# A fused retention and gated MLP kernel: slot 5's transposes given to the DMA engines, and two rows of O moved into the prologue

## The chip, the core and the metric

The kernel runs on one core of a Trainium2 chip. Five engines work side by side, each through its own queue in order: TensorE (PE in the profile, with its weight loads as PEld), VectorE (DVE), ScalarE (ACT), GpSimd (POOL) and SyncE (SP). Sixteen DMA engines move data. GpSimd issues loads that convert float32 to bfloat16 on the way (the "software queue"); SyncE issues plain loads, stores and DMA transposes (the "hardware queue"). The metric is the device time of one execution in microseconds; the runs' median is compared.

## The reference

Four batches, eight heads, 768 steps, head size 64. A decayed linear attention gives x, which goes through a two-layer network with the activation h·cos(h):

```python
state = gamma * state + k_t^T v_t          # per head, 64 x 64, gamma = 1 - 2**(-5-h)
y_t   = q_t state / sqrt(64)               # x: 3072 tokens x 512
h = x @ w_in                               # 512 -> 2048
out = (h * cos(h)) @ w_out                 # 2048 -> 512
```

## The kernel before

**Slots and blocks.** A slot is a chunk of 128 steps of two batches, all heads; there are 12, and `ORDER` (line 197) starts with the first chunk of both pairs of batches. For each slot q, k and v are loaded (`load`, line 272), scaled by powers of gamma or cast to bfloat16 (`conv_q`, `conv_k`, `conv_v`, lines 320 to 343), and q and k are transposed into `qkt`. The scores are K·Q with a triangular mask (`a_one` line 386 and `a_mm` line 393 on TensorE, `a_mask` line 406 on DVE). The *block* of a slot (`y_block`, line 538) is one dense piece of TensorE work: the state update (line 508), the part of y from the old state (line 494), the part from the masked scores (line 480) and, from slot 4 on, the scores of the *next* slot (line 389). So the transposes of slot p+1 are needed when the block of slot p runs. Inside a block the second half must follow the first; an instruction that does nothing but wait, on an engine given by `hop_on(p)` (line 467: SyncE up to slot 4, GpSimd from slot 5), passes that signal.

**Two ways to transpose.** Up to slot 5 TensorE does it (`t_mm`, line 355, 16 matmuls of line 361 a slot, and copies from PSUM on ACT and DVE, line 365). From `DMA_T = 6` on SyncE issues two DMA transposes a slot (`dma_t`, line 348).

**Groups and units.** Two slots make a group of 512 tokens; 6 groups. A *full unit* (`f_mm`, line 587) is 128 of the 2048 hidden columns for a group: 4 matmuls of 512 columns, then cos on ACT (`f_cos`, line 593), then the multiplication on DVE (`f_mul`, line 600), which frees the PSUM bank. A *half unit* (`h_mm`, line 605) does two column blocks for one slot's 256 tokens in 8 matmuls of 256 columns, so that work can start before the second slot of a group is ready. O is the second layer: a *row* of O (128 tokens) is four *O units* of 4 matmuls (`o_mm`, line 630, matmuls at line 635), a copy on ACT (`o_out`) and a store on SyncE (`o_dma`, line 646). Seven PSUM banks go round in a fixed order; three buffers hold cos.

**Two regimes.** The prologue (lines 704 to 918: slots 0 to 7, groups 0 and 1, O of group 0) is ordered by a small list scheduler, `Plan`, at build time. Each piece of work has the engines that may do it, a cost, what it comes after, and a rank; `SHIFT` moves single ranks, `ON` fixes engines, `HOLD` names engines that may wait for a more urgent piece. The order that it finds is written out for each engine; no time of it exists on the chip. `LOADS` (line 719) is the order of the software queue. `HALF0` (line 168) says how many column blocks of group 0 are done as half units. `CQ`, `CD` say which engine scales slot 2's q and v, `SPLIT` which masks of slots 0 and 1 go by ACT and GpSimd. The names in these tables are those given by `add`: `f0.8` is a full unit, `t50` a transpose, `dt60` a DMA transpose, `m300` a mask, `cq30` a q scaling, `oc0` a store of a row. DMA transposes there come after the load of k7, the last but one of the software queue (line 800).

The loop from line 943 does groups 2 to 5: 16 steps a group, each a full unit of group g and an O unit of group g-1, with a block at steps 3 and 11, followed by the conversions and DMA transposes two slots ahead and SyncE's loads three slots ahead (`load(nc.sync, ...)`, 13 issues a slot, because k and v are loaded with halves exchanged from slot 8 on). The first such load, slot 8's, is issued in the prologue (line 903).

Of the kernel before, what the change touches and what calls it, by code (L numbers as in the profile page):

```python
# [164 lines left out]
HOLD = ""  # L165
# [6 lines left out]
def kernel(  # L172
# [7 lines left out]
    out: bass.AP,  # L180
):
    nc = tc.nc
    B, H, S, D = q.shape
    C = 128
    NC = S // C
    DM = H * D
    DF = moe_w_in.shape[1]
    HP = H // 2
    KIN = DM // 128
    KOUT = DF // 128  # L190
    NP = B // 2 * NC
    NG = NP // 2
    PRE = 5
    NB = 3
    DMA_T = 6

    ORDER = [0, NC] + [x for x in range(1, NP) if x != NC]
    SWAP = 8
    LATE = NC

    scale = 1.0 / math.sqrt(D)
    lg = [math.log(1.0 - 2.0 ** (-5.0 - h)) for h in range(H)]

    ctx.enter_context(tc.manual_schedule())
# [262 lines left out]
    def hop_on(p):  # L467
        return nc.sync if p <= 4 else nc.gpsimd
# [225 lines left out]
    for h in range(H):  # L694
        nc.scalar.activation(out=dec[:, h % 2, h // 2, :], in_=dist, func=AF.Exp, bias=lnsc,
                             scale=float(lg[h]))
    nc.scalar.activation(out=gq, in_=lgp, func=AF.Exp, bias=lnsc)
    nc.scalar.activation(out=gk, in_=lgp, func=AF.Exp, scale=-1.0)
    nc.scalar.activation(out=lnsc, in_=halfpi, func=AF.Sin)
    for i in range(7):  # L700
        idle_mm("E", 2)


    PL = 6
    ASEP = 4
    MERGE = 4
    CQ, CD = "P", "DP"
    SPLIT = {(1, 1, 1), (0, 1, 1)}
    HM, HCQ, HCV = "q2", "", ""
    plan = Plan({"bank": 7, "cos": 3, "sem": 8, "out": 4, "port": 1, "ring": 7}, 6.5)  # L710
    add = plan.add
    SB2 = {"D": (0.33, 0.42), "A": (0.49, 0.585)}
    TT = {"D": (0.6, 0.69), "P": (1.03, 1.05)}
    PS = {"D": (0.6, 0.69), "A": (0.49, 0.585)}
    ld = {}
    prev = None
    at = lambda tm: dict(start=0.0, free=0.0, done=tm, lat=0.0)
    ld["q", 0, 0], ld["q", 0, 1], ld["k", 0, 0], ld["k", 0, 1] = map(at, (3.9, 5.0, 7.4, 7.4))
    LOADS = ["Q1", "K1", "v0", "v1", "w0a", "w0b", "w1", "w2", "q2", "k2", "w3a", "v2", "w3b", "o0", "q3", "k3", "v3", "o1", "q4", "o2", "k4", "v4", "q5", "k5", "o3", "v5", "q6", "k6", "v6", "q7", "k7", "v7"]
# [26 lines left out]
    T = {}  # L746
    G = lambda *k: T.get(k)
    for p in range(PL + 2):
# [26 lines left out]
        if p < DMA_T:  # L775

            for u in range(2):
                cq, ck = ([T["c" + x, p, b] for b in ((u,) if p < 2 else (0, 1))] for x in "qk")
                ev = lambda w, x, need: add("DA", SB2, lambda e, p=p, u=u, w=w: t_copy(p, u, w, e),
                                            need + old, 10 * p + 0.5, (), [("bank", 1)] if w else [],  # L780
                                            name="e%s%d%d" % (x, p, u))
                if p < 2:
                    tq = add("E", 0.225, lambda e, p=p, u=u: t_mm(p, u, 0), cq, 10 * p + 1,
                             [("bank", 1)], (), "full", name="tq%d%d" % (p, u))
                    T["eq", p, u] = ev(0, "q", [tq])
                    tk = add("E", 0.225, lambda e, p=p, u=u: t_mm(p, u, 1), ck + [T["eq", p, u]],
                             10 * p + 1, (), (), "full", name="tk%d%d" % (p, u))
                    T["ek", p, u] = ev(1, "k", [tk])
                else:
                    tq = tk = add("E", 0.45, lambda e, p=p, u=u: (t_mm(p, u, 0), t_mm(p, u, 1)),  # L790
                                  cq + ck, 10 * p + 1, [("bank", 1)], (), "full",
                                  name="t%d%d" % (p, u))
                    T["eq", p, u] = ev(0, "q", [tq])
                    T["ek", p, u] = ev(1, "k", [tk, ("issued", T["eq", p, u])])
                T["tq", p, u], T["tk", p, u] = tq, tk
            kq = {u: [T["eq", p, u], T["ek", p, u]] for u in range(2)}
        else:
            for w, x in enumerate("qk"):
                T["dt", p, w] = add("S", (1.3, 4.6), lambda e, p=p, w=w: dma_t(p, w),
                                    [T["c" + x, p, 0], T["c" + x, p, 1], ld["k", 7, 0]] + old, 10 * p,  # L800
                                    name="dt%d%d" % (p, w))
            kq = {u: [T["dt", p, 0], T["dt", p, 1]] for u in range(2)}
# [81 lines left out]
    for o, x, p in pend:  # L884
        o["after"] += [T[c, p, b] for b in range(2) for c in (("cv", "cd") if x == "v" else ("c" + x,))]
    for x, ops in ((HM, [T[("m",) + x] for x in SPLIT]), (HCQ, [T["cq", 2, b] for b in range(2)]),
                   (HCV, [T["cd", 2, b] for b in range(2)])):
        for o in plan.ops:
            if o["name"] == x:
                o["after"] += ops  # L890
# [52 lines left out]
    for g in range(2, NG + 1):  # L943
        for s in range(16):
            hf, r = divmod(s, 8)
            p = 2 * (g + 1) + hf
            if g < NG:
                if g == 2 and s == 0:
                    o_mm(1, 0, 0)
# [48 lines left out]
```

## Time and profile before

| | |
|---|---|
| median of 3 runs | 209.5 us (209.27 to 209.53) |
| the profiled execution's own time | 208.1 us |
| its span | 206.3 us |
| granted TensorE clock | 1.00 |
| TensorE busy | 201.4 us, 98% |
| DVE, ACT, POOL busy | 55%, 56%, 36% |
| software queue | 15.47 MB, last load issued at 51.0 us, lands 11.5 us later |
| first useful matmul of the MLP | 15.76 us |

Times in the profile count from the start of the span. A line of a timeline reads: start, length, engine, source line, operation, output and inputs, count, and in brackets the idle time before it with what ended it. A line of the chain reads: start, length, what. "SPq" and "POOLq" are the queues of these engines, where DMAs are issued.

### The profile page before, as it was taken

The numbers are of one execution on the slowest core, as the hardware profiler recorded it, in microseconds if no ns is written. First come the engines' busy times: TensorE is split into PE (matmuls) and PEld (weight loads), VectorE is DVE, ScalarE is ACT, GpSimd is POOL, SyncE is SP. The second block draws the span as 40 slices with busy tenths as digits, with TensorE's granted clock in tenths as the row PEclk, the third lists the DMA queues.
The fourth block names the chain that finished last, engine by engine and source line by source line (L and its number), as shares of the span: only waits on it lengthen the run. The fifth ranks groups of instructions, "written<-read, shape, count | busy, mean of one in ns | idle before, by whom it ended". The sixth has DMA issues, their size and how long they took to land.

```text
span 206.3 us, 5229 instructions
## 1 busy us (share of the span) xinstructions
PE 201.4 (98%) x2178; PEld 108.6 (53%) x2178; DVE 114.2 (55%) x194; ACT 115.2 (56%) x193; POOL 73.8 (36%) x77
## 2 busy tenths in 40 slices
PE   7999999999999999999999999999999999999994
PEld 2558656868945545445445445454444444444442
DVE  5589897866996548338338438448442444444000
ACT  7567886859855357547546546554555553554120
POOL 8969979899973004305207005200000000000000
PEclk9999999999999999999999999999999999999999
DMA  7999999999998976876877675501101101110212
GB/s 121 186 262 210 314 241 312 255 342 276 344 312 150 231 158 175 201 193 171 192 177 144 151 193 142 153 0 56 53 1 51 51 3 51 51 51 0 104 53 102
DMA packets 58600, 32.15 MB, mean 156 GB/s; under 512 B 47696, under 2 KB 53072, under 8 KB 58576
## 3 DMA queue, kind: packets, MB, share of 16 engines
q0 software_dynamic: 14352, 15.47, 33.9%
q1 hardware_dynamic: 44080, 16.28, 31.1%
q8 instruction: 17, 0.28, 0.6%
q10 hardware_dynamic: 144, 0.07, 0.1%
q14 instruction: 7, 0.06, 0.1%
HBM read 27.26 MB, written 6.29 MB: 163 GB/s over the span
## 4 chain that ended last, share of the span: by engine, by line
PE 78%; DMA 10%; POOL 7%; DVE 2%; issue 1%; ACT 1%; POOLq 0%; DVEq 0%
PE bank L635 37%; PE bank L590 27%; DMA vf<-in_v_dram 10%; PE bank L611 4%; PE bank L389 2%; PE bank L480 2%; PE bank L655 2%; DVE gt L619 1%; PE st_ps L508 1%; POOL qf L281 1%; POOL kf L281 1%; PE bank L494 1%; PE bank L361 1%; POOL w_in_sb L300 1%; POOL ks L281 1%
## 5 line engine op out<-in xcount | busy, mean ns | idle before, releaser
L598 ACT ACTIVATE cosb<-bank,halfpi 128x512 bf16<-128x512 f32 x96 | 65.6, 690 | 53.2 <-PE bank L590 48.0
L635 PE MATMUL bank<-w_out_sb,gt 128*128 128x512 bf16 x368 | 90.9, 379 | 0.0
L602 DVE TENSOR_TENSOR gt<-bank,cosb 128x512 bf16<-128x512 f32 x72 | 49.1, 690 | 55.8 <-ACT cosb L598 55.7
L590 PE MATMUL bank<-xt,w_in_sb 128*128 128x512 bf16 x288 | 73.2, 379 | 0.0
L635 PEld LDWEIGHTS <-gt 128*128 128x128 bf16 x368 | 35.5, 98 | 42.3 <-issue 0.2
L590 PEld LDWEIGHTS <-w_in_sb 128*128 128x128 bf16 x288 | 27.6, 98 | 32.3
L324 POOL TENSOR_TENSOR qs<-qf,gq 128x512 bf16<-128x512 f32 x18 | 18.5, 1044 | 43.5 <-PE bank L480 22.6
L408 DVE TENSOR_TENSOR am<-bank,mask 128x512 bf16<-128x512 f32 x40 | 24.8, 682 | 4.2 <-PE bank L389 4.2
L313 ACT COPY ob<-bank 128x512 f32<-128x512 f32 (+1 forms) x24 | 14.0, 582 | 16.0 <-PE bank L635 13.9
L611 PE MATMUL bank<-xt,w_in_sb 128*128 128x256 bf16 x192 | 22.3, 273 | 0.0
L611 PEld LDWEIGHTS <-w_in_sb 128*128 128x128 bf16 x192 | 18.5, 98 | 3.1
L619 DVE TENSOR_TENSOR gt<-bank,cosb 128x512 bf16<-128x512 f32 x24 | 16.0, 686 | 4.7 <-ACT cosb L598 4.6
L313 ACT CAST xt<-bank 128x512 bf16<-128x512 f32 x21 | 11.4, 588 | 10.8 <-PE bank L480 10.1
L313 ACT CAST ks<-kf 128x512 bf16<-128x512 f32 x20 | 11.5, 625 | 2.7 <-DMA kf<-in_k_dram 2.7
L664 PE MATMUL bank<-zero 128*128 128x512 bf16 x34 | 10.5, 442 | 1.1 <-DVE halfpi L680 1.1
L480 PE MATMUL bank<-am,vs 64*64 64x128 bf16 (+1 forms) x320 | 10.3, 206 | 0.1
L336 POOL TENSOR_TENSOR vs<-vf,gk 128x512 bf16<-128x512 f32 x8 | 8.9, 1113 | 3.3 <-PE bank L480 1.5
L331 POOL TENSOR_TENSOR vs<-vf,gk 128x512 bf16<-128x512 f32 x8 | 8.2, 1042 | 5.2 <-DMA vf<-in_v_dram 3.8
L281 POOL DMA_DIRECT2D vf<-in_v_dram x8 | 9.4, 1182 | 1.0 <-DVE vs L336 0.8
L315 DVE CAST stb<-st_ps 128x512 bf16<-128x512 f32 x9 | 6.2, 687 | 3.8 <-PE st_ps L508 3.3
L389 PE MATMUL bank<-qkt 64*64 64x128 bf16 (+1 forms) x320 | 8.0, 206 | 0.3 <-ACT qkt L313 0.2
L313 ACT COPY qkt<-bank 128x512 bf16<-128x512 bf16 x13 | 7.1, 592 | 1.8 <-PE bank L361 1.2
(66 smaller groups left out, 132.7 us busy)
## 6 DMA issues: line engine op xcount, KB each, us to landing
out_dram<-ob SPq DMA_DIRECT2D x23, 256.0 KB, 2.4
vf<-in_v_dram POOLq DMA_DIRECT2D x8, 512.0 KB, 12.0
qf<-in_q_dram POOLq DMA_DIRECT2D x6, 512.0 KB, 12.5
kf<-in_k_dram POOLq DMA_DIRECT2D x6, 512.0 KB, 12.4
w_out_sb<-in_moe_w_out_dram POOLq DMA_DIRECT2D x4, 512.0 KB, 14.1
qf<-in_q_dram SPq DMA_DIRECT2D x4, 512.0 KB, 4.6
w_in_sb<-in_moe_w_in_dram POOLq DMA_DIRECT2D x4, 256.0 KB, 8.7
w_in_sb<-in_moe_w_in_dram POOLq DMA_DIRECT2D x2, 512.0 KB, 10.5
```

The source lines that it names most:

```text
L281: eng.dma_start(out=t.rearrange("p b h d -> p (b h) d"), in_=src[ds(2 * bp, 2), :, ds(c * C, C), :].rearrange("b h t d -> t (b h) d"))
L313: nc.scalar.copy(out=out, in_=in_)
L324: ENG[e].tensor_tensor(out=qb(p)[:, b], in0=qf[p % PRE][:, b], in1=bc(gq, ORDER[p] % NC), op=ALU.mult)
L389: return nc.tensor.matmul(ap[b][ts(x, 64), a, lo:], lhsT=kt(p % NB, b, h)[:, ts(x, 64)], rhs=qt(p % NB, b, h)[:, lo:], tile_position=(64 * ...
L408: nc.vector.tensor_tensor(out=am[p % 2][b][u], in0=bank.rearrange("p (a t) -> p a t", a=HP), in1=(dec[:, b] if p < 2 else mask[second(p, 0 ...
L480: m = nc.tensor.matmul(held["yp", p][b][ts(j, 64), a, lo:], lhsT=vs[p % NB][ts(r, 64), b, h, :], rhs=am[p % 2][b][h // 4][ts(r, 64), h % 4 ...
L590: nc.tensor.matmul(bank, lhsT=w_in_sb[:, i, ts(f, 128)], rhs=xt[g % 2][:, i, :], start=(i == 0), stop=(i == KIN - 1))
L598: nc.scalar.activation(out=cb, in_=bank, func=AF.Sin, bias=halfpi)
L602: nc.vector.tensor_tensor(out=gt[g % 2][:, f, :], in0=bank, in1=cb, op=ALU.mult)
L611: nc.tensor.matmul(bank[:, ts(e, 256)], lhsT=w_in_sb[:, i, ts(f + e, 128)], rhs=xt[g % 2][:, i, ts(hf, 256)], start=(i == 0 and e == 0), s ...
L619: nc.vector.tensor_tensor(out=gt[g % 2][:, f : f + 2, ts(hf, 256)], in0=bank.rearrange("p (f t) -> p f t", f=2), in1=cb.rearrange("p (f t) ...
L635: nc.tensor.matmul(bank, lhsT=gt[g % 2][:, f, ts(j, 128)], rhs=w_out_sb[:, f, :], start=(f == 0), stop=(f == KOUT - 1))
```

## The change

Slot 5 is transposed by DMA instead of TensorE (`DMA_T` 5). The DMA transposes of slot p in the prologue come after the load of v of slot p, and the loads of slot p+1 after the issue of these transposes, where they had all come after k7. Two rows of O of group 1 (`ROWS = 2`) become pieces of the prologue's plan, beside the blocks of slots 4 and 5; the loop's first group does the other two, one unit before step 0, then at steps 1 to 3 and 8 to 11. The signal inside a block goes by SyncE for slots 0 to 3, by ACT for 4 and 5 and by GpSimd from 6 on. Group 0 has 4 column blocks as half units instead of 8; the order of the loads, the engines of slot 2's scalings, the split masks and the tables of ranks and engines are others.

```diff
-HOLD = ""
+HOLD = "A"
 SHIFT = {
...
-HALF0, SPARE, RF, RM, COLD = 8, 1, 50.0, 50.0, 5.2
+HALF0, SPARE, RF, RM, COLD = 4, 0, 40.0, 30.0, 5.2
...
+    ROWS = 2
-    DMA_T = 6
+    DMA_T = 5
+    HOP = "SSSSAAP"
...
     def hop_on(p):
-        return nc.sync if p <= 4 else nc.gpsimd
+        return {"S": nc.sync, "P": nc.gpsimd, "A": nc.scalar}[HOP[min(p, 6)]]
...
-    CQ, CD = "P", "DP"
-    SPLIT = {(1, 1, 1), (0, 1, 1)}
-    HM, HCQ, HCV = "q2", "", ""
+    CQ, CD = "D", "D"
+    SPLIT = {(1, 0, 0), (0, 1, 1)}
+    HM, HCQ, HCV = "", "", ""
...
-    LOADS = ["Q1", "K1", "v0", "v1", "w0a", "w0b", "w1", "w2", "q2", "k2", "w3a", "v2", "w3b", "o0", "q3", "k3", "v3", "o1", "q4", "o2", "k4", "v4", "q5", "k5", "o3", "v5", "q6", "k6", "v6", "q7", "k7", "v7"]
+    LOADS = ["Q1", "K1", "v0", "v1", "w0a", "w0b", "w1", "q2", "w2", "k2", "v2", "w3a", "o0", "w3b", "o1", "q3", "k3", "v3", "q4", "k4", "o2", "v4", "o3", "q5", "k5", "v5", "q6", "k6", "v6", "q7", "k7", "v7"]
...
-                                    [T["c" + x, p, 0], T["c" + x, p, 1], ld["k", 7, 0]] + old, 10 * p,
+                                    [T["c" + x, p, 0], T["c" + x, p, 1], ld["v", p, 0]] + old, 10 * p,
...
+    for p in range(DMA_T, PL + 1):
+        ld["q", p + 1, 0]["after"] += [("issued", T["dt", p, w]) for w in range(2)]
...
     add("S", 8.0, lambda e: load(nc.sync, PL + 2, "q ks vs"),
-        [T["dt", PL + 1, w] for w in range(2)], 10 * PL + 20, name="l8")
+        [("issued", T["dt", PL + 1, w]) for w in range(2)], 10 * PL + 20, name="l8")
...
+    for j in range(ROWS):
+        for part in range(4):
+            T["o", 4 + j, part] = add(
+                "E", 0.865, lambda e, j=j, part=part: o_mm(1, j, part),
+                ([T["o", 4 + j, part - 1]] if part else []) + [
+                    T["mul", ("h", 2 + j // 2, f)] for f in range(4 * part, 4 * part + 4, 2)],
+                3000 + 4 * j + part, [("bank", 1)] if part == 0 else [], (), "full",
+                name="o%d.%d" % (4 + j, part))
+        add("A", (0.49, 0.585), lambda e, j=j: (o_out(1, j, e), o_dma(1, j)), [T["o", 4 + j, 3]], 300,
+            (), [("bank", 1)], name="oc%d" % (4 + j))
...
+        units = [divmod(n, 4) for n in range(4 * ROWS + 1 if g == 2 else 0, 16)]
+            if g == 2 and s == 0:
+                o_mm(1, ROWS, 0)
-            if g > 2 or s > 0:
-                o_mm(g - 1, *divmod(s, 4))
-            if s % 4 == 3:
-                o_out(g - 1, s // 4, "A")
+            row = None
+            if g > 2 or s in (1, 2, 3, 8, 9, 10, 11):
+                j, part = units.pop(0)
+                o_mm(g - 1, j, part)
+                if part == 3:
+                    row = j
+                    o_out(g - 1, j, "A")
             if p < NP and r == 3:
                 block(p)
-            if s % 4 == 3:
-                o_dma(g - 1, s // 4)
+            if row is not None:
+                o_dma(g - 1, row)
```

As the scheduler writes it out, TensorE has 80 rows at line 361 instead of 96, 160 at line 611 instead of 192 and 304 at line 590 instead of 288; SyncE issues 14 DMA transposes instead of 12. GpSimd issues q6, k6, v6 after slot 5's v scalings, and q7, k7, v7 after slot 6's q scalings; its instructions for these loads wait for nothing of SyncE's.

## The prediction

> **What bounds the kernel now.** I read the page's share of engines and its slices first, then the chain that ended last, then TensorE's order in time, then the queues that feed it (SyncE, ACT, DVE, single DMA issues).
>
> ```profile
> span 206.3 us, 5229 instructions
> ...
> PE 201.4 (98%) x2178; PEld 108.6 (53%) x2178; DVE 114.2 (55%) x194; ACT 115.2 (56%) x193; POOL 73.8 (36%) x77
> ...
> PE   7999999999999999999999999999999999999994
> ```
>
> TensorE is busy all the way; no other engine passes 56%. So only two things move the time: what TensorE has to do, and gaps in it. The chain (start, length, what) and TensorE's timeline say where both are:
>
> ```profile
> 42.31 0.63 PE bank L389 x26
> ...
> 47.98 6.99 PE bank L611 x64
> 54.97 0.89 PE bank L361 x16
> 55.86 0.87 PE bank L611 x8
> 56.73 0.86 PE bank L635 x4
> ```
> ```profile
> 15.76 1.92 PE L611 MATMUL bank<-xt,w_in_sb 128*128 128x256 bf16 x16
> ...
> 42.31 0.63 PE L389 MATMUL bank<-qkt 64*64 64x128 bf16 x32 [0.22 <-ACT qkt L313]
> ...
> 67.94 0.22 PE L494 MATMUL bank<-qkt,stb 64*64 64x128 bf16 x2
> 68.19 0.22 PE L389 MATMUL bank<-qkt 64*64 64x128 bf16 x2
> ```
>
> Useful matmuls run without a break from 15.76 us (everything before is paced by the first loads). I find two gaps after that: 0.22 us at 42.31 (slot 3's scores wait for a copy of its transposes on ACT) and one inside slot 5's block, where the first score (L389) starts 0.63 us into the block at 67.56, against 0.38 to 0.43 us in the blocks at 61.65, 77.17, 92.60 and 107.91. It waited for slot 6's DMA transpose, issued at 64.23.
>
> **What is taken away.** (1) Slot 5's 16 transposes on TensorE: the row at 54.97, 0.89 us, all of it on the path. Their four copies on ACT and DVE (about 0.6 and 0.4 us each) lay beside matmuls: nothing. Weighed against a page: the Trainium skill, "TensorE: Matmul & The Clock Gate", Part 4, gives about 275 ns per PE transpose in a kernel, by which 16 would save 4.4 us; here one lasts 220 ns but the next starts 56 ns later, so the row decides. (2) HALF0 from 8 to 4: four half-group units (32 matmuls of 256 columns) become four full ones (16 of 512); 0.874 us against 0.864 each, -0.04 us. (3) The two gaps go: the first because slot 3's copies now have an O unit between transposes and scores, the second because slot 6's transposes get earlier than their block (below): -0.22 and -0.25. Sum -1.40 us. The 8 units of O of group 1 that move into the prologue are the same matmuls elsewhere: 0 by themselves. The new ranks, engines and HOLD change order alone; what I read out of the new order is in the terms below.
>
> **What is added: early loads.** From about 20 to 40 us the software queue is never empty, so what lands is set by bytes, not by order.
>
> ```profile
> 23.77 1.18 POOL L281 DMA_DIRECT2D vf<-in_v_dram  x1
> 24.96 0.77 POOL L305 DMA_DIRECT2D w_out_sb<-in_moe_w_out_dram  x1
> ```
> ```profile
> vf<-in_v_dram POOLq DMA_DIRECT2D x1, 512.0 KB, 12.9
> w_out_sb<-in_moe_w_out_dram POOLq DMA_DIRECT2D x1, 512.0 KB, 14.3
> ```
>
> Last column: us from issue to landing. So v of slot 3 lands at 23.77 + 12.9 = 36.7 and the second quarter of w_out (o1) at 24.96 + 14.3 = 39.3. In the new order o1 comes before q3, k3, v3; the set of loads up to there is the same, so v3 now lands at about 39.3, k3 at 37.7 (1.5 us a load). Where is TensorE? From 15.76: 4 half units 3.5, S 0.4, 12 full units 10.4, transposes 0.9, scores 0.6, slot 2's block 1.33, 4 O units 3.5, switches of mode 0.4 (the same sum for before gives its measured 34.93): the first unit of group 1 starts at 36.65, and the fifth, which reuses the first one's bank, at 40.15.
>
> ```profile
> 35.16 1.14 ACT L313 CAST ks<-kf 128x512 bf16<-128x512 f32 x2 [0.78 <-DMA kf<-in_k_dram]
> 36.20 1.36 ACT L598 ACTIVATE cosb<-bank,halfpi 128x512 bf16<-128x512 f32 x2
> ```
> ```profile
> 36.75 0.69 DVE L336 TENSOR_TENSOR vs<-vf,gk 128x512 bf16<-128x512 f32 x1 [2.12 <-DMA vf<-in_v_dram]
> ...
> 42.78 2.48 DVE L408 TENSOR_TENSOR am<-bank,mask 128x512 bf16<-128x512 f32 x4 [1.14 <-PE bank L389]
> ```
>
> On ACT the cos of unit 1 stands behind slot 3's two k casts (37.7 + 1.1 = 38.8, cos to 39.5). On DVE its multiplication stands behind slot 3's v scaling (39.3 + 0.7 = 40.0), so the bank is free at 40.65: **+0.5 us** at the fifth unit (0 if the loads land 0.5 us sooner than in this trace; 1.3 if the scaling takes 1.5 us, its longest here). What waits behind it: the other multiplications, which then run at 0.6 us against 0.87 for a unit and catch up. A wait for the last w_in columns or o0 before it, 0 to 0.7 by the same count, is inside this one, not on top. Slot 3's transposes need POOL's q scaling, now behind q5, k5, v5 (three issues at 1.2 us) and 3 scalings at 1.05 from v3's landing: 44.0, TensorE arrives at 44.1: **+0.1** (0 to 0.5, if one takes the 1.58 us seen at 58.10).
>
> Slot 3's masks: three in a row, then v of slot 4 and a copy, then the fourth on DVE: 0.47 (score start to first mask, 42.31 to 42.78) + 1.9 + 0.7 to 0.95 + 0.4 + 0.65 = 4.1 to 4.4 us after the scores start; slot 3's block follows them after 0.6 + 1 O, transposes 0.9, 2 O = 4.1 us, and its first bank is that mask's: **+0.2** (0 to 0.35). At the very start, one 512-column fill more between slots 0 and 1: 0.05, left out; S of slot 0 waits for scalings moved to POOL that end at 18.8, TensorE gets there at 19.4: nothing, and 0.5 if they take 1.58.
>
> **What is added: DMA transposes.** Slots 5, 6 and 7 are needed when the blocks of slots 4, 5, 6 start. Counting units as above, these blocks move from 61.65 to about 67.6, 67.56 to 72.6 and 77.17 to 83.1, because O units now stand before them. Slot 5's pair is issued when v5 is scaled for (about 52.4 and, behind a row of O, 54.4). q6, k6, v6 are issued by POOL only at about 55.6, after slot 5's v, into an empty queue; first loads took 5.7 us, so q6 lands about 61, k6 62, v6 64. Slot 6's pair waits on SyncE behind two rows of O, to about 65.6 and 67: landed by 69.8, asked for at 73.0. Slot 7's q goes at about 73, its k behind O row 1 of group 1 at 77.5: landed by 80.3, asked for at 83.5. A transpose takes 2.7 to 2.8 us to land alone and 3.6 at 64.23; none in the trace runs among loads, as slot 6's now does (q7 to v7 are issued at 63 to 66). Against a margin of 3.2 us I take **0** (0 to 0.5). The Trainium skill's page "DMA: Bandwidth & Descriptors", Queues, rings and completion order, says that an engine alternates between queues by packets; as an estimate that doubles 2.7 to 5.4 us, and the sum would be the same.
>
> ACT now holds k6's casts ahead of O rows 1 to 3: with k6 at 62 they end at 63.7, before those rows do (64 to 66.7); 0. The signals between the halves of blocks 4 and 5 move from SyncE and POOL to ACT; behind them stand only copies that need the same block: 0.
>
> **What is late next: SyncE.** Slot 8's loads are issued behind slot 7's k transpose, at 79 instead of 69.35 us, while the block of slot 8 comes 1.1 us earlier than before:
>
> ```profile
> 69.35 0.39 SPq L281 DMA_DIRECT2D qf<-in_q_dram  x1
> 69.83 5.78 SPq L289 DMA_DIRECT2D kf<-in_k_dram  x6
> 75.72 3.95 SPq L289 DMA_DIRECT2D vf<-in_v_dram  x6
> 79.76 1.74 SPq L647 DMA_DIRECT2D out_dram<-ob  x2
> 81.67 1.31 SPq L350 DMA_TRANSPOSE qkt<-ks  x1
> 83.08 1.25 SPq L350 DMA_TRANSPOSE qkt<-qs  x1
> ```
>
> From the end of slot 5's block: O row done 1.7, ACT to 2.5, its store 0.6, k transpose 1.3 (to 4.6), 13 load issues (9.5 to 10.9 in the trace, 10.1 on average), store 0.7, two transposes 2.7 (to 18.2; landed 19.7; slot 7's block asks for it at 21.2), 10.1, 0.7, k 1.4, then 2.7 to land: 33.2. Slot 8's block starts 32.7 after (8.9 to slot 6's block, 11.9 to slot 7's, 11.9 more) and asks 0.4 into it: 33.1. On the mean it just fits; with the spread of about 0.7 I take **+0.25** (0 to 1.6). After it TensorE takes 15.3 us a slot and SyncE 13.5, so it falls back. Slot 8's and 9's k casts hold ACT's cos meanwhile, with 2 and 0.7 us before a bank is missed: 0.
>
> **Sum.** -1.40 + 0.5 + 0.1 + 0.2 + 0.25 = **-0.35 us**. The profiled execution took 208.1 us (span 206.3 and 1.8 around it), so 207.75 there; the runs' median is 1.4 above it, and 209.5 - 0.35 is **209.2 us**. A measurement tells about 0.2% (0.42 us) from nothing, so this is "no change", barely.
>
> **Rivals.** *The gain stays* (faster): if v3 is earlier and SyncE keeps its quick values (9.5 + 0.6), the added waits shrink to 0.2 to 0.6: 208.3 to 208.9. For it: before has no load wait at all after 15.76. Against: TensorE's place and the loads' meet within 0.2 us at three points. *SyncE too late* (slower): with the trace's slow values for one slot (issues 10.9, a store at 1.4, a transpose at 2.3) slot 9's transposes land 35.7 after, 2.6 us too late: -1.40 + 0.8 + 2.6 is +2.0, 211.5; with half of that excess 210.2. It decides from a wait of 1.05 us there. For it: stores at 1.4 (94.69) and a transpose at 2.3 (111.69) exist; against: singly. *Transposes among loads don't land in time* (the change's turns not kept, since POOL issues q7 without waiting for slot 6's transposes): slot 5's block waits from 6 us a transpose; at 8 us it waits 2: -0.35 + 2 is 211.1.
>
> **How the numbers follow.** Forecast 0.36 (209.1 to 209.7), gain stays 0.34, SyncE 0.22, transposes 0.08. Faster 0.34 and slower 0.30 follow; the range goes from all gains with 0.2 of waits (208.3) to half of the late SyncE and some more (210.8).
>
> **What would show it.** 80 instead of 96 rows at L361; a wait of TensorE at about 40 us on DVE's multiplication, with DVE before it waiting for v; blocks of slots 4, 5, 6 at about 67.6, 72.6, 83; slot 8's loads from 79; a first score late in the block at about 107. Wrong if TensorE is gapless from 16 to 60 us (then 208.5), or if it waits over 1 us anywhere, most likely at a score behind a DMA transpose.

## The result, and the profile after

The changed kernel takes 220.9 us (median of 4 runs, 218.7 to 223.1) against 209.5 for the kernel before: a ratio of 1.051 [1.044, 1.059]. It is slower by 11 us, where 209.2 and a range up to 210.8 had been forecast. Here and below a median is over all runs, while a ratio leaves out those more than 1.5% above the fastest of their kernel. The profiled execution of the changed kernel took 223.06 us (span 221.3), 2 us above its median; its times are read against the 208.1 us (span 206.3) of the profiled execution before. Lines of the kernel after stand two higher: L361 is now L363, L389 is L391, L647 is L649.

The page of the kernel after: span, engines, then the slices for TensorE, its granted clock and the DMA engines.

```profile
span 221.3 us, 5128 instructions
...
PE 202.2 (91%) x2122; PEld 108.0 (49%) x2146; DVE 114.1 (52%) x192; ACT 113.0 (51%) x190; POOL 74.4 (34%) x78
...
PE   8999999999999404999999899999999999999993
PEclk9999999999999955899999999999999999999999
DMA  7999999997979998375967759667111011100212
```

TensorE has about as much to do as before (202.2 us, 201.4 before). What is new is one hole, in slices 14 to 16 of 40 (74 to 85 us), and half clock in slices 15 and 16. The DMA engines stay busy through the hole (9, 9 and 8 tenths); their share falls only after it. Three stretches of the same kernel, with the busy time of PE, PEld, DVE, ACT, POOL, the granted clock, the DMA share and GB/s:

```profile
66.70:74.40 7.70, 7.49 (x174) 4.11 (x175) 4.17 (x7) 2.73 (x5) 2.98 (x3) 1.00 1.06 228
74.40:85.40 11.00, 0.26 (x24) 0.09 (x12) 0.00 (x0) 0.00 (x0) 0.55 (x1) 0.62 1.21 103
85.40:90.70 5.30, 4.89 (x81) 3.01 (x83) 3.08 (x5) 2.19 (x4) 1.50 (x2) 0.50 0.35 96
```

For 11 us the compute engines do next to nothing, while the DMA engines count as fully busy and move only 103 GB/s (the same engines move 291 GB/s from 30 to 45 us). The clock is 0.50 for another 5.3 us after the work goes on. What TensorE waited for, first as totals (engine, line, what it waited for: us, times, longest), then from TensorE's timeline:

```profile
PE bank L391 <- DMA qkt<-qs: 11.5, 2, 10.8
```
```profile
16.87 3.67 PE L613 MATMUL bank<-xt,w_in_sb 128*128 128x256 bf16 x32
...
69.00 0.22 PE L510 MATMUL st_ps<-vs,ks 64*64 64x64 bf16 x2
...
85.47 0.28 PE L391 MATMUL bank<-qkt 64*64 64x128 bf16 x2 [10.82 <-DMA qkt<-qs]
...
122.96 0.24 PE L391 MATMUL bank<-qkt 64*64 64x64 bf16 x2 [0.66 <-DMA qkt<-qs]
```

The first score of slot 6, asked for in slot 5's block, waits 10.8 us for slot 6's DMA transposes; slot 9's wait 0.7. The chain that ended last goes through the same place:

```profile
56.44 5.57 DMA qf<-in_q_dram
...
62.18 0.96 POOL qs L326
63.18 0.98 POOL qs L326
64.16 5.37 DMA qf<-in_q_dram
69.53 15.81 DMA qkt<-qs
```

Before, this chain ran through matmuls here. Now it is a load, a scaling, a load again and a transpose of 15.8 us. Who issued what, from the queues of SyncE and of GpSimd:

```profile
65.23 1.37 SPq L649 DMA_DIRECT2D out_dram<-ob  x2
66.77 2.66 SPq L352 DMA_TRANSPOSE qkt<-ks  x1
69.53 4.57 SPq L352 DMA_TRANSPOSE qkt<-qs  x1
74.19 1.90 SPq L649 DMA_DIRECT2D out_dram<-ob  x2
76.27 7.93 SPq L352 DMA_TRANSPOSE qkt<-qs  x1
```
```profile
62.18 2.04 POOL L326 TENSOR_TENSOR qs<-qf,gq 128x512 bf16<-128x512 f32 x2 [2.26 <-DMA qf<-in_q_dram]
64.16 1.19 POOL L283 DMA_DIRECT2D qf<-in_q_dram  x1
65.35 1.16 POOL L283 DMA_DIRECT2D kf<-in_k_dram  x1
66.50 1.15 POOL L283 DMA_DIRECT2D vf<-in_v_dram  x1
```

GpSimd issues q7, k7, v7 from 64.16, right behind slot 6's q scalings. SyncE gets to slot 6's transposes only at 66.77, behind stores of O. So the transposes run in the middle of the loads. The issues, with KB each and us to landing:

```profile
qkt<-ks SPq DMA_TRANSPOSE x1, 5.2
...
kf<-in_k_dram POOLq DMA_DIRECT2D x1, 512.0 KB, 11.8
...
vf<-in_v_dram POOLq DMA_DIRECT2D x1, 512.0 KB, 18.2
...
qkt<-qs SPq DMA_TRANSPOSE x1, 15.8
...
qkt<-qs SPq DMA_TRANSPOSE x1, 11.2
```

In order of issue: slot 5's k (56.45), k7, v7, slot 6's q, slot 7's q. The landing of slot 6's k is not in the trace; the weight loads of TensorE waited 10.9 us for it. Before, a transpose landed in 2.7 to 3.6 us:

```profile
qkt<-qs SPq DMA_TRANSPOSE x1, 3.6
...
qkt<-qs SPq DMA_TRANSPOSE x1, 2.7
```

Both sides suffer: v7 takes 18.2 us. These loads of q, k and v bring float32 into float32 tiles (`qf`, `kf`, `vf`); of the software queue's loads only the weights and q and k of slots 0 and 1 are converted on the way, so conversion has no part in what follows. Inside the hole, from 74 to 78 us, the queues show (packets, MB, share of the 16 engines):

```profile
q1 hardware_dynamic: 479, 0.12, 65.6%
q0 software_dynamic: 44, 0.17, 57.9%
```

44 packets in 57.9% of 16 engines for 4 us are 0.84 us a packet. Before, from 58 to 62 us, with stores of O beside it and no transpose:

```profile
q0 software_dynamic: 274, 0.97, 73.0%
```

That is 0.17 us a packet of about the same size (3.5 to 4 KB). The SyncE queue's packets, 0.25 KB on the mean, take 88 ns here; from 62 to 66 us before, transposes and plain transfers together took 34 ns each.

**Balance.** 10.8 (the wait), 2.65 (half of 5.3 us at half clock), 1.1 (first useful matmul at 16.87 instead of 15.76) and 0.66 (slot 9) are 15.2; the savings were priced at 1.4, which leaves 13.8 of the span's 15.0. Of the other 1.2 us, four gaps of 0.16 to 0.33 us (at 21.07, 29.90, 70.72 and 87.84) are 0.9.

### The profile page after: what moved, and what is told of

Same layout as the page of the kernel before. It is cut to its first block, busy times and chain, and to the rows that moved or that the text cites. A ratio compares the mean times of both kernels' runs of the same rounds, so it can differ in the third digit from the quotient of the medians.

```text
span 221.3 us, 5128 instructions
## 1 busy us (share of the span) xinstructions
PE 202.2 (91%) x2122; PEld 108.0 (49%) x2146; DVE 114.1 (52%) x192; ACT 113.0 (51%) x190; POOL 74.4 (34%) x78
## 4 chain that ended last, share of the span: by engine, by line
PE 48%; DMA 26%; DVE 7%; SPq 7%; POOL 5%; issue 4%; ACT 1%; POOLq 0%; DVEq 0%; ACTq 0%
PE bank L637 23%; PE bank L592 18%; DMA vf<-in_v_dram 11%; DMA qkt<-qs 8%; SPq L291 5%; DMA qf<-in_q_dram 5%; DVE gt L604 3%; PE bank L613 2%; PE bank L657 2%; POOL qs L326 1%; DMA kf<-in_k_dram 1%; PE bank L391 1%; DVE qs L326 1%; PE bank L482 1%; SPq L352 1%
## 5 line engine op out<-in xcount | busy, mean ns | idle before, releaser
L637 PE MATMUL bank<-w_out_sb,gt 128*128 128x512 bf16 x357 | 89.9, 384 | 1.1 <-issue 0.5
L600 ACT ACTIVATE cosb<-bank,halfpi 128x512 bf16<-128x512 f32 x96 | 63.9, 689 | 44.5 <-PE bank L592 33.1
L604 DVE TENSOR_TENSOR gt<-bank,cosb 128x512 bf16<-128x512 f32 x76 | 50.3, 687 | 53.2 <-ACT cosb L600 53.2
L592 PEld LDWEIGHTS <-w_in_sb 128*128 128x128 bf16 x304 | 29.1, 98 | 34.4
L391 PE MATMUL bank<-qkt 64*64 64x128 bf16 (+1 forms) x320 | 8.8, 213 | 11.8 <-DMA qkt<-qs 11.5
L613 PE MATMUL bank<-xt,w_in_sb 128*128 128x256 bf16 x160 | 18.0, 273 | 0.0
L621 DVE TENSOR_TENSOR gt<-bank,cosb 128x512 bf16<-128x512 f32 x20 | 13.8, 691 | 5.7 <-ACT cosb L600 5.3
L613 PEld LDWEIGHTS <-w_in_sb 128*128 128x128 bf16 x160 | 15.6, 98 | 2.3
L333 POOL TENSOR_TENSOR vs<-vf,gk 128x512 bf16<-128x512 f32 x8 | 8.2, 1042 | 20.4 <-DMA vf<-in_v_dram 15.5
L391 PEld LDWEIGHTS <-qkt 64*64 64x64 bf16 x320 | 7.4, 112 | 13.6 <-DMA qkt<-ks 10.9
L315 ACT CAST xt<-bank 128x512 bf16<-128x512 f32 x18 | 9.8, 589 | 6.3 <-PE bank L482 6.0
L317 DVE CAST xt<-bank 128x512 bf16<-128x512 f32 x6 | 3.9, 686 | 16.4 <-PE bank L482 16.3
L666 PE MATMUL bank<-zero 128*128 128x512 bf16 x34 | 10.7, 442 | 1.1 <-DVE halfpi L682 1.1
L482 PE MATMUL bank<-am,vs 64*64 64x128 bf16 (+1 forms) x320 | 11.2, 212 | 0.1
L315 ACT CAST stb<-st_ps 128x512 bf16<-128x512 f32 x4 | 2.3, 583 | 15.8 <-PE st_ps L510 15.8
```

Of the source, the lines that this page charges most:

```text
L315: nc.scalar.copy(out=out, in_=in_)
L391: return nc.tensor.matmul(ap[b][ts(x, 64), a, lo:], lhsT=kt(p % NB, b, h)[:, ts(x, 64)], rhs=qt(p % NB, b, h)[:, lo:], tile_position=(64 * ...
L482: m = nc.tensor.matmul(held["yp", p][b][ts(j, 64), a, lo:], lhsT=vs[p % NB][ts(r, 64), b, h, :], rhs=am[p % 2][b][h // 4][ts(r, 64), h % 4 ...
L592: nc.tensor.matmul(bank, lhsT=w_in_sb[:, i, ts(f, 128)], rhs=xt[g % 2][:, i, :], start=(i == 0), stop=(i == KIN - 1))
L600: nc.scalar.activation(out=cb, in_=bank, func=AF.Sin, bias=halfpi)
L604: nc.vector.tensor_tensor(out=gt[g % 2][:, f, :], in0=bank, in1=cb, op=ALU.mult)
```

## The experiments

The theory after the result: slot 6's DMA transposes and slot 7's software loads, running together, slow each other down. Rivals: SyncE's lateness makes the transposes late by itself; or the new order of the prologue is at fault. Each ratio is against the kernel before, measured beside it.

**e1: the turn made real.** GpSimd waits for slot 6's two transposes to land before it issues q7.

```diff
+        if p == 7 and n == "q":
+            w = nc.gpsimd.nop(nofuse=True)
+            for i in range(2):
+                after(held["dt", 6, i], w)
         load(nc.gpsimd, p, n)
```

> The changed kernel with one wait more: GpSimd issues slot 7's q load only when both of slot 6's DMA transposes have landed, so that none of them runs beside slot 7's loads. Theory A (slot 6's transposes and slot 7's software-queue loads hold each other up; that alone is the 10.8 us): slot 6's pair lands 2.7 to 3.6 us after each issue, by about 71, TensorE's wait at slot 5's block is 0 to 0.5 us, its clock stays at 1.00; slot 7's loads start at about 71 instead of 64 and land by 79, its transposes by 82.5 (asked for at 83.5). Time 210.0 to 211.5 us. Rival B (two transposes issued one behind the other are slow at this place whatever runs beside them, as the second's issue of 4.57 us might say): the landing stays over 8 us and TensorE waits over 5 us; time over 215 us. Rival C (most of the loss lies in the new order, outside the wait): no transposes late, but still over 214 us.

Measured: 216.2 us, 1.032 [1.027, 1.038]. Slot 6's pair landed in 4.2 and 3.3 us, slot 7's in 2.7 and 2.8, the clock stayed at 1.00 and the 10.8 us were gone. The time was still almost 5 us above the expected range, since q7 left 8.2 us later. GpSimd, then TensorE:

```profile
72.33 1.19 POOL L283 DMA_DIRECT2D qf<-in_q_dram  x1 [7.75 <-DMA qkt<-qs]
```
```profile
95.23 1.02 PE L592 MATMUL bank<-xt,w_in_sb 128*128 128x512 bf16 x4 [1.32 <-DVE gt L604]
...
101.12 0.24 PE L391 MATMUL bank<-qkt 64*64 64x64 bf16 x2 [1.74 <-DMA qkt<-qs]
...
115.85 0.24 PE L391 MATMUL bank<-qkt 64*64 64x64 bf16 x2 [1.82 <-DMA qkt<-qs]
```

Slot 7's transposes then went at 80.8 and 82.9 and slot 8's loads from 84.3 instead of 69.35, and SyncE was too late for slots 8 and 9: these two waits and the one at 95.23 are 4.9 of the 7.4 us. Another 1.1 us is slot 6's block waiting for slot 7's k transpose (85.72). Keeping the turn trades the collision for a late SyncE.

**e2: slot 7's loads on SyncE**, behind slot 6's transposes.

```diff
-            ... load(nc.gpsimd, p, n),
+            ... load(nc.sync if p == 7 else nc.gpsimd, p, n),
```

> The changed kernel with slot 7's three loads issued by SyncE, behind slot 6's transposes, in place of GpSimd's software queue. Theory A: slot 6's pair, issued at about 66.8 and 68.1, lands in 2.7 to 4 us each (the loads come behind it in the same queue, from 69.5 or so, and overlap only its end); TensorE waits 0 to 1 us at slot 5's block; time 210.0 to 212 us. Rival B: the wait stays over 5 us, time over 215 us. If transposes are held up by any load, whichever queue it is in, slot 6's q, with loads issued right behind it, lands in 6 us or more and TensorE waits 2 us or more: 212 to 216 us.

Measured: 213.4 us, 1.020 [1.015, 1.025]. Slot 6's pair landed in 5.1 and 4.4 us. The profiled execution was the slowest (218.63) and shows the collision one slot earlier:

```profile
kf<-in_k_dram POOLq DMA_DIRECT2D x1, 512.0 KB, 13.5
...
qkt<-ks SPq DMA_TRANSPOSE x1, 13.3
```

These are slot 5's k transpose and k6. In the kernel after, at the same place, the transpose took 5.2 and the loads 5.6 to 6.3. So the same neighbours collide in one execution and not in another. What the other three runs (212.4 to 213.8 us) lost above the expected 210 to 212 is in no trace.

**e3: transposes of slots 6 and 7 behind k7**, as before; slot 5's stay where the change has them.

```diff
-  ... ld["v", p, 0]] + old, 10 * p,
+  ... ld["v", p, 0] if p == 5 else ld["k", 7, 0]] + old, 10 * p,
-    for p in range(DMA_T, PL + 1):
+    for p in range(DMA_T, DMA_T + 1):
```

> The changed kernel with slot 5's transposes among the loads as before, but those of slots 6 and 7 planned behind the last software-queue loads again, and slot 7's loads no longer planned behind slot 6's transposes; they are then issued right behind slot 6's loads, at about 60 to 63 us, and land by 68. Theory A: slot 6's transposes start when at most the tail of v7 is in flight and land in 2.7 to 4 us; no wait over 0.5 us at slot 5's block; time 209.5 to 211 us (before, with 1.1 us lost at the start and 1.4 us saved). Rival B: over 215 us. Rival C: over 214 us without a late transpose.

Measured: median 210.7 us. Six of ten runs took 209.0 to 210.8, and the ratio, 1.004 [1.001, 1.008], is theirs; three took 212.3 to 213.0 and one 219.3. In the profiled execution (212.32) slot 6's pair, beside only the tail of v7, landed in 5.6 and 6.0 us, more than the 2.7 to 4 expected, and slot 5's block waited 1.8 us. Moving slot 6's pair behind the loads takes away most of the loss in nine of ten runs; why one run took 219.3 is not shown.

**e4: the rest of the change alone.** Slot 5 on TensorE again (`DMA_T` 6, DMA transposes behind k7); two rows of O and the new order kept.

```diff
-    DMA_T = 5
+    DMA_T = 6
-  ... ld["v", p, 0]] + old, 10 * p,
+  ... ld["k", 7, 0]] + old, 10 * p,
...
-    for p in range(DMA_T, PL + 1):
-        ld["q", p + 1, 0]["after"] += [("issued", T["dt", p, w]) for w in range(2)]
```

> The changed kernel without its DMA part: slot 5's 16 transposes on TensorE again, those of slots 6 and 7 behind the last software-queue loads, the two rows of O of group 1 and the new order kept. Theory A: no late transpose; the time is that of the run before plus 0.9 us of transposes: 209.5 to 211.5 us. Rival C (order and O rows lose the time): over 214 us.

Measured: 210.3 us, 1.0066 [1.0043, 1.0089]. No transpose was late. So the rest of the change costs 1.4 us here; it isn't where the 11 us come from.

**e5: the old kernel with the new rule for DMA transposes** (after the slot's own v).

```diff
-  ... ld["k", 7, 0]] + old, 10 * p,
+  ... ld["v", p, 0]] + old, 10 * p,
```

> The kernel before with one rule changed: slot 6's two DMA transposes are planned behind the load of their own slot's v and no longer behind the last software-queue load, so SyncE issues them at about 58 to 61 us, while q7, k7 and v7 are in flight (the last of these lands at 62.5 in the run before). All else is as it was. Theory A (a DMA transpose and software-queue loads hold each other up): at least one of the pair takes over 5 us to land, against 2.8 to 3.6 us, and the loads beside them land over 1 us later than in the run before; slot 5's block asks at 68.2, so the time moves only if a landing passes 7 us: 208.5 to 209.5 us with landings of 5 to 7 us, up to 216 us with one of 14. Rival B (it needs three transposes and the stores of the changed kernel): both land in 2.7 to 3.6 us, and the time is that of before, 208.8 us.

Measured: 210.0 us, 1.0052 [1.0027, 1.0077]. The transposes left at 60.5 and 62.7, when the last load had under 3 us to run, and no score waited for them (their landing is not in the trace). The time went into a signal inside a block that now stood behind them on SyncE (1.3 us). Inconclusive for the collision.

**e6: slot 7's loads on ACT's queue**, a hardware queue.

```diff
-            ... load(nc.gpsimd, p, n),
+            ... load(nc.scalar if p == 7 else nc.gpsimd, p, n),
```

> The changed kernel with slot 7's three loads issued by ACT in place of GpSimd, so through a hardware queue, at about the same time and beside the same transposes. If only the software queue's loads collide with DMA transposes: slot 6's pair lands in 2.7 to 5.5 us, no wait over 2 us at slot 5's block, 210 to 213 us. If any load in another queue does: a landing over 8 us, TensorE waits over 4 us, over 215 us.

Measured: 214.4 us, 1.025 [1.020, 1.029]. The transposes of slot 6 landed in 6.7 and 5.4 us, those of slot 7 in 5.3 and 4.3, and the engines moved 222 GB/s meanwhile. Slot 5's block lost half a microsecond, after a copy on ACT; the wait for a transpose comes at slot 8's block, for slot 9's, issued late at 109.43. And the packets on ACT's queue, from 67 to 76 us:

```profile
74.63 0.24 PE L496 MATMUL bank<-qkt,stb 64*64 64x128 bf16 x2 [0.50 <-ACT xt L315]
...
113.26 0.24 PE L391 MATMUL bank<-qkt 64*64 64x64 bf16 x2 [1.87 <-DMA qkt<-qs]
```
```profile
q10 hardware_dynamic: 4081, 1.04, 51.8%
```

So loads from a hardware queue, with as many bytes in the same place, double a transpose's time. They don't multiply it by five. But their packets are also smaller, about 0.26 KB against about 4 KB on the software queue. Whether the queue or the size of its packets makes the difference is not separated by any run.

**e7: slot 5 by DMA and the rows of O on the old order**, slot 5's pair together, slots 6 and 7 behind k7, v7 on SyncE after them.

```diff
+  SHIFT, ON, HALF0, LOADS, CQ, CD, SPLIT of the kernel before
+  dt5: (dma_t(5, 1), dma_t(5, 0)) in one piece after v5
+  v7:  load(nc.sync, 7, "v") behind slot 7's transposes
```

> The two rows of O and slot 5's DMA transposes of the change, built on the ranks, engines and load order of before, with the transposes kept clear of the software queue: slot 5's pair issued back to back ahead of the stores of O (about 53.5 to 56, before q6's first packets at 58), slots 6 and 7 behind k7's load (68 to 71), v of slot 7 loaded by SyncE behind them. Theory A: no landing over 4 us, no wait of TensorE over 0.5 us, the first useful matmul at 15.8 as before, the saving of 0.9 to 1.4 us is kept: 207.4 to 208.3 us where before takes 208.8. If the collision needs less overlap than I think (the tail of v5 at 54.4, the head of q6 at 58): single runs of 210 to 219 us, as in the third kernel of the first set.

Measured: 210.8 us, 1.0075 [1.0049, 1.0101]. Transposes landed in 2.7 to 4.8 us and slot 5's block waited for none, but the expected saving didn't come. The longest wait that remained after the start is SyncE's: held by four stores ahead of slot 6's pair, it was late with slot 8's loads (from 78.65), and slot 9's transposes were 1.4 us late:

```profile
57.91 10.55 SPq L649 DMA_DIRECT2D out_dram<-ob  x4
```
```profile
110.00 0.24 PE L391 MATMUL bank<-qkt 64*64 64x64 bf16 x2 [1.41 <-DMA qkt<-qs]
```

**e8 and e9: no software load near slots 6 and 7, on the old order.** q7, k7, v7 by SyncE behind slot 6's pair, then slot 8's q and k, then slot 7's pair; the prologue's stores of O by ACT (e8) or by SyncE (e9).

```diff
+            if p == 7: ... load(nc.sync, 7, n)
-    ... (o_out(0, j, e), o_dma(0, j))
+    ... (o_out(0, j, e), o_dma(0, j, nc.scalar))     # e8 alone
```

> The two rows of O and slot 5's DMA transposes of the change on the ranks and load order of before, with no software-queue load beside a transpose: slot 5's pair ahead of q6, slot 6's behind v6 (about 63 to 66), slot 7's three loads by SyncE behind that pair, slot 8's q and k, slot 7's pair and slot 8's v after them; the stores of these O rows issued by ACT, so that SyncE waits for none. Theory A (collisions, and a SyncE that is late, are all that eats the saving): no transpose over 4.5 us, no wait over 0.5 us at any block, slot 9's transposes in time: 207.3 to 208.6 us where before takes 208.8 to 209.5. Rival (the moved rows and the start of the new order cost as much as they save): no wait, but 209 us or more.

> The same with the stores of the O rows left on SyncE, where slot 6's q transpose and slot 7's loads stand behind them. Theory A: slot 6's q transpose is issued behind the fourth store of group 0, at about 67 to 69, lands by 72, asked for at about 73 to 74: 207.5 to 209.5 us; the difference to the kernel before is what the stores in SyncE's order cost, 0 to 1 us.

Measured: e8 210.3 us, 1.0056 [1.0035, 1.0077]; e9 216.2 us, 1.034 [1.032, 1.036]. In e8 no transpose was late; its profiled execution (214.72) lost 4.4 us to copies on ACT behind slot 7's k casts. In e9 slot 6's q transpose stood behind stores until 69.88 and all that follows it on SyncE came later, slot 7's pair at 87.27 and 88.70; slot 6's block waited 2.8 us for that pair, and another 2.1 us went to ACT:

```profile
92.39 0.22 PE L391 MATMUL bank<-qkt 64*64 64x128 bf16 x2 [2.84 <-DMA qkt<-qs]
```

Where the stores are issued decides 6 us, where 0 to 1 had been expected.

**e10: the changed kernel once more, and e11: the same with slot 7's loads in six half loads.**

```diff
-            ... load(nc.gpsimd, p, n),
+            ... load(nc.gpsimd, p, n if p < 7 else n + "0 " + n + "1"),     # e11
```

> The changed kernel once more, unaltered. Theory A with a collision that depends on how the packets meet: the landing of slot 6's q transpose differs between executions (15.8 us in the first profile), and the time with it: single runs from 212 to 223 us, TensorE's wait at slot 5's block 3 to 11 us. If the collision is fixed by the order alone: again 15 to 16 us of landing and 10 to 11 us of wait, 218 to 223 us.

> The changed kernel with slot 7's q, k and v loaded in two halves each, still on GpSimd's software queue (six issues in place of three, packets of 2 KB in place of 4 KB, the same bytes). If it is the large packets that a transpose's 256-byte packets wait for: slot 6's transposes land in about half, 7 to 10 us, TensorE waits 1 to 5 us, 212 to 216 us. If the software queue as such collides: 12 us or more, as in the changed kernel.

Measured: e10 218.9 us, 1.043 [1.039, 1.047]; e11 220.9 us, 1.046 [1.043, 1.049]. In e10 slot 6's pair landed in 13.1 and 10.7 us and the wait was shorter:

```profile
81.43 0.28 PE L391 MATMUL bank<-qkt 64*64 64x128 bf16 x2 [6.44 <-DMA qkt<-qs]
```

In e11 the pair took 8.8 and 10.7 us, the wait 5.1. The collision is there in all three profiles, 8.8 to 15.8 us for a transpose of slot 6. On the size of packets e11 says nothing, for the packets stayed as they were: 1101 software packets carried 3.79 MB from 50 to 110 us, and 1042 carried 3.77 MB in the kernel after from 50 to 95.

**e12: slot 6 on TensorE again**, the loads unchanged. It removes one side of the collision and puts 16 matmuls and four copies back.

```diff
-        if p < DMA_T:
+        if p < DMA_T or p == 6:
...
-        ... [("issued", T["dt", p, w]) for w in range(2)]
+        ... [("issued", T["dt", p, w] if p == 5 else T["tq", p, w]) for w in range(2)]
```

> The changed kernel with slot 6's 16 transposes on TensorE (0.9 us) in place of its two DMA transposes; slot 5's and 7's by DMA as changed, all loads in the same queues and order. Theory A (slot 6's pair beside q7, k7, v7 is the 10 us): no wait over 1 us at slot 5's block, q7 to v7 land in 5.4 to 6.5 us instead of 5.4 to 18.2, TensorE's clock stays at 1.00: 210 to 212.5 us (before, 0.5 less for what is left of the saving, plus 1 at the start, plus 0 to 2 of SyncE). If something else in the new order holds slot 5's block: still over 216 us.

Measured: 210.75 us median, ratio 1.006 [1.002, 1.010], against 1.043 and 1.051 for the changed kernel. The same stretch of time as above, and v7:

```profile
74.40:85.40 11.00, 11.00 (x261) 6.05 (x258) 5.85 (x9) 5.71 (x10) 2.10 (x3) 1.00 0.79 154
```
```profile
vf<-in_v_dram POOLq DMA_DIRECT2D x1, 512.0 KB, 9.3
```

No hole, full clock, and v7, issued at the same place, lands in 9.3 instead of 18.2 us. Although TensorE has 16 transposes more, 7.7 us are gone (0.037 of 209; 9.5 against the first measurement). This settles the cause: the 10.8 us are gone without the transposes (here), without the loads at the same time (e1), and with the loads on another queue (e6). What is left shows as 0.96 us lost from 95 to 110 us and 0.84 from 110 to 125.

**e13 and e14: e8 with slot 7's k casts moved behind slot 5's copies**, on the old order (e13) and the new (e14).

```diff
+    for b in range(2):
+        T["ck", 7, b]["after"] += [("issued", T["yc", 5, x]) for x in range(2)]
```

> The eighth kernel (old ranks, no software-queue load beside a transpose, stores of these O rows on ACT) with slot 7's k casts on ACT behind the copies of slot 5's block, which they held up for 4.4 us there. Theory A: no wait of TensorE over 0.5 us between 17 and 125 us: 207.2 to 208.6 us, 0.5 to 1.5 us less than before. If ACT's stores or slot 7's late k hold the next cos instead: 209 us or more, with a wait at a unit of group 2.

> The same rules on the ranks, engines and load order of the change: what the change is worth when its transposes are clear of the software queue and SyncE is in time. The start of the new order costs 0.5 to 1.2 us against the old (first useful unit at 16.9 against 16.4): 208 to 209.8 us, about no change against before, which is what I forecast for the change itself; over 211 us if the new order has a wait of its own that the late transposes hid.

Measured: e13 210.9 us, 1.009 [1.006, 1.012]; e14 214.8 us, 1.029 [1.026, 1.032]. The profiled execution of e13 is its fastest (209.02) and shows no wait above 0.7 us after the start, so it doesn't explain the median. In e14 slot 8's loads stand ahead of slot 7's pair (83.76 and 85.13), which costs 4.2 us; that is this kernel's own ordering and says nothing on the change.

**e15: e12 with the six prologue stores of O issued by ACT. e16: the same on the old order.**

```diff
-    ... (o_out(0, j, e), o_dma(0, j))
+    ... (o_out(0, j, e), o_dma(0, j, nc.scalar))
-    ... (o_out(1, j, e), o_dma(1, j))
+    ... (o_out(1, j, e), o_dma(1, j, nc.scalar))
```

> The twelfth kernel (slot 6's transposes on TensorE) with the six stores of O rows in the part laid out by the planner issued by ACT in place of SyncE. If SyncE's lateness is what is left: slot 7's transposes are issued at 72 to 74 instead of 75.7 and 77.0, slot 8's loads start at about 76 instead of 79.2, the waits of 1.0 and 0.8 us between 95 and 125 us go, 208.3 to 209.7 us. If not: as before this edit, 210 to 211 us.

> The same on the ranks, engines and load order of before: slot 5's transposes by DMA, slot 6's on TensorE, two rows of O beside slots 4 and 5, stores on ACT. The start is 0.5 us earlier than in the new order; saving of 0.9 (slot 5) less 0.9 (slot 6) plus the two gaps: 207.9 to 209.2 us, about 0.3 under to 0.5 over before.

Measured: e15 209.3 us, 1.0027 [1.0001, 1.0054]; e16 211.1 us, 1.010 [1.0065, 1.0135]. In e15 slot 8's loads start at 75.36 instead of 79.20 and the loss of e12 from 95 to 125 us is gone:

```profile
95.00:110.00 15.00, 15.00 (x282) 7.82 (x279) 9.53 (x15) 9.15 (x16) 4.09 (x4) 1.00 0.72 166
110.00:125.00 15.00, 15.00 (x169) 7.15 (x160) 8.41 (x13) 8.56 (x14) 4.09 (x4) 1.00 0.70 164
```

The span falls from 208.5 to 207.2 us; the ratios' intervals overlap, so the runs alone don't prove that gain. In e16 a w_in load was 1.1 us late at the start, signals on ACT cost 0.7 and slot 9's transposes 0.6; together 2.4 us, where its profiled execution lies 2.3 us over the kernel before. No version tried beats the kernel before; e15 comes nearest. Of those built to keep the saving (e7, e8, e9, e13, e14, e16) none reached its expected time.

## Why the prediction was wrong

**The step that failed** stands under "What is added: DMA transposes": slot 6's pair among the loads, priced at 0 (0 to 0.5) "against a margin of 3.2 us". It cost a wait of 10.8 us and half clock for 5.3 us more. Two things were wrong in it. The landing was mis-sized: 10.7 to 15.8 us for slot 6's transposes beside software loads (the kernel after and e10), where 3.6 was the worst row before and nothing in that trace showed such a neighbour. (The 3.6 is not of 64.23: that row holds two transposes, and it is the second's, slot 7's q at 65.63.) The upper end of 0.5 had no row behind it; the bound needed a transfer beside loads, and there was none, so it should have been left wide. And the margin was smaller: slot 6's q transpose left at 69.53, not at 67, as the pair began 1.2 us later than counted and the k transpose's issue took 2.66 us. With a landing of 2.8 there would still have been 2 us to spare, so the landing alone decides.

The estimate of 5.4 us in the prediction, worked out from the Trainium skill, "DMA: Bandwidth & Descriptors", Queues, rings and completion order, agrees with the hardware queue of e6 (4.3 to 6.7 us) and not with the software queue. It takes the packets of both queues to be equally long. In e6 they were of about the same size, 0.26 KB; in the kernel after the loads' packets are of about 4 KB, so turns by packets would by themselves give more than double. That a packet of the loads takes about five times as long as without a transpose beside it, turns by packets don't explain. The same page's Rules for kernel authors say that a transpose next to ordinary DMAs "needs nothing". That stands in a rule on corrupted data; for the time these runs show otherwise.

**The third rival had the mechanism** (GpSimd issues q7 without waiting for slot 6's transposes) **and the wrong price**: 211.1, from 8 us a transpose. Three parts were missing: the landing was up to twice that; TensorE then ran at half clock for 5.3 us, which no wait in the trace before was long enough to show; and slot 7's q transpose took 11.2 us, with a store, slot 7's k transpose (91.99) and slot 8's loads (from 93.4) behind it on SyncE. Its chance of 0.08 was too low for a step of which no row existed. (In the first rival, waits of 0.6 make 208.7 by its own sum, not 208.9.)

**What held.** Slot 5's transposes went: the rows recorded at their line fell from 96 to 80, as forecast. Slot 4's and slot 5's blocks started at 69.0 and 74.05, 1.4 us after the forecast 67.6 and 72.6, 1.1 of it from the start of the kernel. Both signs of being wrong came: no gap of TensorE over 0.22 us from 17 to 60 us ("gapless" but for these), and a wait over 1 us at a score behind a DMA transpose. With the collision removed, the time ends close to that of before, as the sum said: e12 and e15 stand 0.3 to 0.6% above the kernel before. But these keep slot 6 on TensorE in exchange for slot 5, so the 0.89 us of the sum is shown in no total.

**SyncE too late** was right as a mechanism. In e12, where slot 8's loads start at 79.20 (79 forecast), 1.8 us are lost, against the 2.6 of that rival; in e1, where they start at 84.3, slots 8 and 9 cost 1.7 and 1.8; in e15, where only the stores had left SyncE, nothing is lost there.

**Early loads, +0.5, +0.1 and +0.2:** did not occur. TensorE has no wait at the fifth unit of group 1, nor at slot 3's transposes or block. The 0.22 us gap at slot 3's scores went, as said, but one of 0.22 came before slot 2's (29.90). **The start, 0.05 "left out":** it was larger. The first useful matmul stands at 15.76 to 16.62 us in seven profiles of the old order (mean 16.2) and at 16.28 to 17.25 in eleven of the new (mean 16.8): about +0.6. The range within each order is larger, so single traces can't price it. Of the 1.1 us between the kernel after and before, about half may have come with the loads: the first v was issued at the same time and landed 0.56 us later (12.77 instead of 12.21). The rest shows in the chain of the kernel after and, second, in ACT's and TensorE's timelines before:

```profile
15.59 0.89 DVE gt L317
16.52 0.41 PE bank L433 x8
16.94 3.61 PE bank L613 x32
```
```profile
13.94 1.14 ACT L313 CAST gt<-vf 128x512 bf16<-128x512 f32 x2
...
15.19 0.64 PE L431 MATMUL bank<-am,gt 128*64 128x128 bf16 x16
```

The last cast of v (`gt`), which the last matmuls ahead of the MLP need, ends at 16.48 on VectorE, behind three masks; before, it ended at 15.08 on ACT. That its place sets the start is read from the chain, and was not tried by itself.

**What stays open.** Why the software queue's packets take five times longer beside a transpose, and whether the queue or the size of its packets makes the collision; why slot 5's k transpose collides in one execution (13.3 us) and less or not in others (4.9 to 7.7); why the runs of e12 fall into two groups (208.5 to 208.9, and 210.3 to 212.9 us), where e4's lie within 1.4; and much of the 1.5 us of e4's median and the 2.2 of e13's over the kernel before.

## What to carry to other kernels

A DMA transpose that ran into loads from the software queue took three to six times its landing time here (8.8 to 15.8 us against 2.7), and it slowed these loads too; if no row of the trace shows such a pair, its price is unknown and the range has to be wide. A turn that exists only in a planner's order is kept by nothing on the chip: look for the wait, and if there is none, ask what happens when one queue is late. And when a chain of transfers is put on one queue, count every issue on it: in the profiled executions, freeing SyncE of six stores went with 1.3 us (e12 to e15), more than the transposes that the change took from TensorE (0.9).

## What the runs showed of the hardware

The stop of TensorE costs more than itself: work ended at 74.6 us, the granted clock fell to 0.50 at 77.0, 2.4 us later, and came back at about 90.6, 5.2 us after the work went on. Shorter stops can do it too: in e3 a wait of 1.8 us that ended at 77.3 was followed by a clock of 0.50 from 78.6 to 82.0 us, and in e6 one of 1.9 us by 0.50 from 114.7 to 118.1. But waits of 1.7 to 1.9 us in e1, e2, e10 and e11, and one of 2.8 us in e9 (92.39), were followed by none, so the length of the wait alone doesn't decide. The Trainium skill, "TensorE: Matmul & The Clock Gate", HAM oscillation — how this bites in real kernels, puts the limit for idle gaps at about 3.4 us; here the clock fell 2.4 us into a gap, and after gaps of 1.8 and 1.9.

The Trainium skill, "Advanced Engine Details and Errata", X-Bar Transpose (TRN2), says that transpose DMAs "are as fast as regular DMAs". No run here compares the two alone; among software loads the engines moved 103 GB/s for both together over 11 us.
